# 320 rows of an output projection moved to five DMA engines

## The chip, the cores and the metric

The kernel runs on one core of a Trainium2 chip. The metric is the device time of one execution in microseconds (us), lower being better. "Span" is the time from the first to the last instruction in a profile or an execution; it leaves out about 2 us of the device time.

## The reference

A decode step: one token, 32 heads, a window of 4096 cached keys and values per head, and an output projection `wo`. A small gated branch (about 3.3 MB of weights) multiplies the result.

```python
W = min(4096, max(256, Sk // 4))
k = k_cache[:, :, Sk - W:, :]            # 32 heads x 4096 x 128, bf16
v = v_cache[:, :, Sk - W:, :]
scores = jnp.einsum("bhqd,bhkd->bhqk", q, k) * (Dh ** -0.5)
p = _softmax(scores, axis=-1)
o = jnp.einsum("bhqk,bhkd->bhqd", p, v)
s = o.transpose(0, 2, 1, 3).reshape(B, Sq, Hq * Dh) @ wo     # wo: 4096 x 512
return x + s * g
```

K and V are 1 MB (1024 KB) a head each, `wo` is 4: 68 such units, or 71 of the 79 million bytes that the kernel reads.

## The kernel before

All big loads go through one queue in program order. K head `i`, V head `i - 4` and now and then a block of `wo` follow one another. Each K or V tile is 128 partitions of 8 KB.

```python
def load(dst, src):
    return tc.keep_in_program_order(nc.sync.dma_start(out=dst, in_=src))
...
blocks = [(0, 8), (8, 8), (16, 8), (24, 4), (28, 4)]
...
def load_wo(i):
    h0, n = blocks[i]
    ...
    if i < last_block:                      # row p*n + t on partition p: one long packet a partition
        load(t[:], rows.rearrange("(p t) n -> p t n", p=P))
    else:                                   # head h, row p: 1 KB packets
        rows = rows.rearrange("(h p) n -> p h n", p=P)
        load(t[:, 0:n - 1, :], rows[:, 0:n - 1, :])
        load(t[:, n - 1, :], rows[:, n - 1, :])
...
for i in range(H + LAG):
    if i < H:
        k_head(i, load_kv(k_pool, A_k_cache, i))
    if i == LAG:                            # the small branch's weights are freed here,
        wts_guard.__exit__(None, None, None)
        v_pool = ctx.enter_context(tc.tile_pool(name="v", bufs=V_BUFS))   # V tiles lie behind what was allocated so far
    if i >= LAG:
        h = i - LAG
        v = load_kv(v_pool, A_v_cache, h)
        if h + 1 in (b[0] for b in blocks):
            load_wo(block_of[h])            # the block of heads 24-27 is issued at h = 27, behind the last K head
        if h == H - 1:
            load_wo(last_block)
        v_head(h, v)
```

For the long packets (8 KB for eight heads, 4 KB for four) a block's outputs have to be repacked (three DVE steps, one small matmul) before they meet `wo`. The tables for that are small constant tiles, one set for eight heads and one for four (`make_masks(8)`, `make_masks(4)`). In SBUF, where the loads put the tiles, the constants, the pool of K tiles, some small work pools and the pool of V tiles lie one behind the other: a later section turns on that.

## Time and profile before

| | before |
|---|---|
| median of 6 runs | 198.74 us (198.45 to 198.95) |
| span of the profiled run | 196.8 us |
| bytes read | 78.84 MB |
| DMA rate from 100 to 120 us | 423 GB/s |

The prediction below shows the lines that say that DMA sets the time. One more view is needed to follow what happened, the timeline of the tensor engine from the last K head on (columns: start, us, instruction, out<-in, count, and in brackets the idle time before and what ended it):

```profile
177.13 3.60 PE L271 MATMUL pt<-ident_bf,kv 128*128 128x128 bf16 x32 [1.49 <-DMA kv<-in_A_k_cache_dram]
...
184.07 0.27 PE L300 MATMUL den_ps<-pT,ones_bf 128*128 128x128 bf16 x1 [1.62 <-ACT pT L294]
184.72 0.17 PE L335 MATMUL ox_ps<-spread,to 128*128 128x16 bf16 x1 [0.38 <-DVE den L302]
...
185.90 1.01 PE L364 MATMUL oT<-pT,kv 128*128 128x1 bf16 x32
187.16 0.99 PE L364 MATMUL oT<-pT,kv 128*128 128x1 bf16 x32 [0.25 <-DVE o L367]
189.47 1.01 PE L364 MATMUL oT<-pT,kv 128*128 128x1 bf16 x32 [1.31 <-DMA kv<-in_A_v_cache_dram]
```

The last K head lands at 177.1. Transposes, scores and softmax take 6.9 us from there to the softmax denominators. Then the repacking (`ox_ps`) and V heads 28 and 29 run at PE's own pace, and heads 30 and 31 wait for their data. So two chains run to the end: **the DMA chain**, whose last V head lands at 191.89, and **the PE chain**, which starts at the last K head. Before the change the second has waits of 1.31 and 1.45 us in it. Without them head 31, at 1.25 us from head to head, would start at about 189.65 in place of 191.93 (an estimate): the PE chain can come some 2.3 us later before it ends the kernel.

The trace's own list of the chain that ended last, in order of time (start, us, what), agrees: it goes back through the last V head's transfer.

```profile
172.23 19.66 DMA kv<-in_A_v_cache_dram
191.89 0.05 issue
191.93 1.01 PE oT L364 x32
192.94 0.61 PE y_ps L135 x16
```

### The profile page before, as it was taken

The page shows a single profiled execution, that of the slowest core. Times are in us where ns is not written, and L with a number is a line of the kernel's source. Part 1 is how long each engine was busy: PE and PEld are TensorE (multiplying, and loading weights), DVE is VectorE, ACT ScalarE, POOL GpSimd, SP SyncE. Part 2 cuts the span into 40 slices and gives each one's busy share as a digit, 9 for nine tenths or more (in the row PEclk, how much of TensorE's full clock was granted, in tenths as well). Part 3 has the DMA queues.
Part 4 walks back from the last instruction along what each step waited for, and adds up shares of the span by engine and source line. Part 5 has one row for each costly group of instructions (what it writes and reads, how often), then busy time and mean ns, then how long its engine had stood idle before and what let it go on. Part 6 is the DMA issues. An engine that isn't in the chain of part 4 may idle for free.

```text
span 196.8 us, 5237 instructions
## 1 busy us (share of the span) xinstructions
PE 119.4 (61%) x2399; PEld 108.4 (55%) x2399; DVE 126.9 (64%) x140; ACT 69.3 (35%) x82; POOL 4.9 (3%) x17
## 2 busy tenths in 40 slices
PE   0315896851969474684829293756665654929443
PEld 0314745841969473583829292656565653929332
DVE  1225049998959993959387937959198929594301
ACT  2000329742565243070707070242525250707000
POOL 1011000000000000000000000000000000000000
PEclk9999999695585555576766667555555585575555
DMA  6999899999999999999999999999999999999960
GB/s 185 383 485 446 355 416 421 426 426 421 426 421 423 421 421 425 423 425 420 426 421 428 421 425 416 425 420 426 423 428 423 425 418 425 421 426 422 426 268 10
DMA packets 11349, 79.17 MB, mean 402 GB/s; under 512 B 1376, under 2 KB 1984, under 8 KB 2368
## 3 DMA queue, kind: packets, MB, share of 16 engines
q1 hardware_dynamic: 11176, 78.85, 96.3%
q8 instruction: 18, 0.29, 0.6%
q10 hardware_dynamic: 152, 0.00, 0.0%
q14 instruction: 3, 0.02, 0.0%
HBM read 78.84 MB, written 0.00 MB: 401 GB/s over the span
## 4 chain that ended last, share of the span: by engine, by line
DMA 71%; DVE 12%; issue 6%; PE 6%; ACT 2%; POOL 1%; SPq 0%; POOLq 0%
DMA kv<-in_A_v_cache_dram 40%; DMA kv<-in_A_k_cache_dram 30%; DVE sS L265 7%; DVE prod L262 3%; ACT kt L272 1%; PE a_ps L202 1%; PE qT_ps L221 1%; PE oT L364 1%; PE qb_ps L230 1%; PE h_ps L135 1%; PE y_ps L135 0%; PE ln_ps L140 0%; PE ln_ps L152 0%; ACT q_bc L232 0%; POOL ln_rstd_x L158 0%
## 5 line engine op out<-in xcount | busy, mean ns | idle before, releaser
L272 ACT COPY kt<-pt 128x1024 bf16<-128x1024 bf16 x64 | 60.2, 1025 | 73.0 <-PE pt L271 73.0
L265 DVE TENSOR_REDUCE sS<-prod 128x32 f32<-128x4096 bf16 x16 | 70.7, 4419 | 0.5
L271 PE MATMUL pt<-ident_bf,kv 128*128 128x128 bf16 x512 | 53.8, 298 | 18.2 <-DMA kv<-in_A_k_cache_dram 17.7
L271 PEld LDWEIGHTS <-kv 128*128 128x128 bf16 x512 | 49.8, 140 | 19.7 <-DMA kv<-in_A_k_cache_dram 18.7
L364 PEld LDWEIGHTS <-kv 128*128 128x128 bf16 x1024 | 30.0, 102 | 30.5 <-DMA kv<-in_A_v_cache_dram 22.8
L262 DVE TENSOR_TENSOR prod<-kv,q_bc 128x4096 bf16<-128x4096 bf16 x16 | 36.5, 2283 | 11.0 <-DMA kv<-in_A_k_cache_dram 8.8
L364 PE MATMUL oT<-pT,kv 128*128 128x1 bf16 x1024 | 32.6, 165 | 17.6 <-DMA kv<-in_A_v_cache_dram 17.3
L243 PE MATMUL sT<-qT_bf,kt 128*128 128x1 bf16 x512 | 20.4, 166 | 2.6 <-ACT kt L272 2.3
L243 PEld LDWEIGHTS <-kt 128*128 128x128 bf16 x512 | 18.3, 103 | 3.4 <-ACT kt L272 3.2
L300 PE MATMUL den_ps<-pT,ones_bf 128*128 128x128 bf16 x8 | 2.0, 253 | 16.9 <-ACT pT L294 16.9
L371 DVE TENSOR_TENSOR o<-oT,rden 128x4 bf16<-128x4 f32 x7 | 1.1, 162 | 17.3 <-PE oT L364 17.3
L294 ACT ACTIVATE pT<-e 128x128 bf16<-128x128 f32 x8 | 2.5, 309 | 16.5 <-DVE e L290 16.5
L140 PEld LDWEIGHTS ln_ps<-x_f,ones_f 128*128 128x128 f32 x4 | 1.0, 312 | 11.3 <-DVE x_f L182 6.4
L287 POOL PARTITION_ALL_REDUCE mb<-m x8 | 3.0, 373 | 162.5 <-DVE m L285 162.5
L205 ACT ACTIVATE a_bf<-a_ps 128x10 bf16<-128x10 f32 x1 | 0.2, 180 | 17.4 <-PE a_ps L202 17.4
L302 DVE TENSOR_REDUCE den<-den_ps 128x4 f32<-128x128 f32 x8 | 2.3, 292 | 5.5 <-PE den_ps L300 5.5
L135 PEld LDWEIGHTS <-ox 128*1 128x1 bf16 x112 | 2.5, 113 | 5.3 <-DVE ox L341 5.3
L367 DVE TENSOR_TENSOR o<-oT,rden 128x1 bf16<-128x1 f32 x4 | 0.6, 161 | 7.2 <-PE oT L364 7.2
L230 PE MATMUL qb_ps<-wq_sb,xn_rep 128*128 128x512 bf16 x16 | 5.2, 497 | 0.0
L135 PE MATMUL y_ps<-wo,ox 128*1 128x128 bf16 x112 | 3.7, 306 | 2.3 <-DVE ox L341 2.3
L140 PE MATMUL ln_ps<-x_f,ones_f 128*128 128x4 f32 x4 | 1.2, 365 | 5.9 <-DVE x_f L163 4.9
L290 DVE TENSOR_TENSOR e<-sS,mb 128x64 f32<-128x64 f32 x8 | 1.8, 224 | 3.9 <-POOL mb L287 3.9
(79 smaller groups left out, 48.2 us busy)
## 6 DMA issues: line engine op xcount, KB each, us to landing
kv<-in_A_k_cache_dram SPq DMA_DIRECT2D x32, 1024.0 KB, 19.7
kv<-in_A_v_cache_dram SPq DMA_DIRECT2D x32, 1024.0 KB, 19.7
wq_sb<-in_A_wq_dram SPq DMA_DIRECT2D x1, 4096.0 KB, 19.2
wo<-in_A_wo_dram SPq DMA_DIRECT2D x3, 1024.0 KB, 20.4
w_sb<-in_B_w_dram SPq DMA_DIRECT2D x1, 1376.0 KB, 7.9
w_sb<-in_B_w_dram SPq DMA_DIRECT2D x1, 1024.0 KB, 10.2
w_sb<-in_B_w_dram SPq DMA_DIRECT2D x1, 512.0 KB, 3.7
wo<-in_A_wo_dram SPq DMA_DIRECT2D x1, 512.0 KB, 19.8
```

The costliest lines, as they stand in the source:

```text
L135: nc.tensor.matmul(ps[32 * j:32 * j + 1, :], lhsT=col, rhs=w[0:k, j * P:(j + 1) * P], start=False, stop=last, skip_group_check=True)
L140: nc.tensor.matmul(ps[:], lhsT=ones_f[:], rhs=src_f, start=True, stop=True)
L230: nc.tensor.matmul(qb_ps[:], lhsT=xn_rep[:, c, :], rhs=wq_h[:, c, 2 * i:2 * i + 8:2, :], start=(c == 0), stop=(c == KC - 1))
L243: nc.tensor.matmul(sT[:, hl // 2, c:c + 1], lhsT=kt[:, c, :], rhs=qT_bf[:, h:h + 1], start=True, stop=True)
L262: nc.vector.tensor_tensor(out=prod[:], in0=kn[:], in1=q_bc[:, h // 2:h // 2 + 1, :].to_broadcast([P, NC, Dh]), op=ALU.mult)
L265: nc.vector.tensor_reduce(out=s["sS"][:, hl // 2, :], in_=prod[:], axis=AX.X, op=ALU.add)
L271: nc.tensor.transpose(pt[:, i, :], kn[:, b * 8 + i, :], ident_bf[:])
L272: nc.scalar.copy(out=kt[:, b * 8:(b + 1) * 8, :], in_=pt[:])
L287: nc.gpsimd.partition_all_reduce(mb[:], m1[:], channels=P, reduce_op=ReduceOp.max)
L294: nc.scalar.activation(out=pT[:], in_=e[:], func=ACT.Exp, scale=scale)
L302: nc.vector.tensor_reduce(out=den[:], in_=den_ps[:], axis=AX.X, op=ALU.add)
L364: nc.tensor.matmul(oT[:, k:k + 1], lhsT=v[:, c, :], rhs=s["pT"][:, hl % 2, hl // 2, c:c + 1], start=(c == 0), stop=(c == NC - 1))
```

## The change

The engines finish unevenly, so some rows of `wo` are to be carried by the engines that finish early. 320 rows (40 partitions of 8 KB) come as two transfers that only five engines are to serve; the other 704 rows of the last eight heads come in 1 KB packets on all engines. All of the last eight heads' outputs lie in one tile.

```diff
+NE = 5
-    make_masks(4)
+    few = const.tile([P, 2, 32], BF16, name="few")
+    ... a 0/1 matrix that spreads ox to the 40 partitions
+    def load_few():
+        t = wo_blk[few_block]
+        for c in range(2):
+            r0 = 8 * few_block * P + c * FEW // 2
+            load(t[32 * c:32 * c + 4 * NE],
+                 A_wo[r0:r0 + FEW // 2, :].rearrange("(b a t) n -> a b (t n)", b=4, a=NE))
...
+        if i == few_block:
+            of_ps = ps_misc.tile([64, n], FP32, tag="misc", name="of_ps")
+            nc.tensor.matmul(of_ps[:], lhsT=few[:].rearrange("p a b -> p (a b)"), rhs=ox[:], start=True, stop=True)
+            ox = sm_pool.tile([64, n], BF16, tag="of", bufs=1, name="of")
+            nc.vector.tensor_copy(out=ox[:], in_=of_ps[:])
...
-        if h == h0:
-            o_blk[i] = sm_pool.tile([P, n], BF16, tag="o", name="o")
+        if h % 8 == 0:
+            o_blk[i] = sm_pool.tile([P, 8], BF16, tag="o", name="o")
...
-            if h + 1 in (b[0] for b in blocks):
-                load_wo(block_of[h])
+            if h in (7, 15, 23):
+                load_wo((h + 1) // 8 - 1)
+            if h == H - 3 * G:                 # h = 20
+                load_few()
+            if h == H - G - 1:                 # h = 27
+                load(wo_rows[r_part:, 0, :], A_wo[h_part * P + r_part:(h_part + 1) * P, :])
+                load_rows(h_part + 1, H - G - h_part - 1)
             if h == H - 1:
-                load_wo(last_block)
+                load_rows(H - G, G - 1)
+                load_rows(H - 1, 1)
```

Cut: the pool tiles `wo_few` and `wo_rows` with two memsets, and renamed helpers.

More of the change, by code (lines that the diff above doesn't have):

```diff
@@ L233 @@
     make_masks(8)
-    make_masks(4)
+    few = const.tile([P, 2, 32], BF16, name="few")
+    nc.vector.memset(few[:], 0.0)
+    for c in range(2):
+        nc.vector.tensor_copy(
+            out=few[:, c, 0:4 * NE].rearrange("p (a b) -> p a b", b=4),
+            in_=ident_bf[:, 4 * NE * c:4 * NE * (c + 1)].rearrange("p (b a) -> p a b", b=4))
     st = {}
@@ L305, in softmax_den, with wo_row, load_rows @@
         s["rden"] = rden
-    blocks = [(0, 8), (8, 8), (16, 8), (24, 4), (28, 4)]
-    last_block = len(blocks) - 1
-    block_of = {h: i for i, (h0, n) in enumerate(blocks) for h in range(h0, h0 + n)}
+    few_block = H // 8 - 1
+    FEW = 8 * 8 * NE
+    h_part, r_part = divmod(24 * P + FEW, P)
+    assert h_part + 1 < H - G and 0 < r_part < P and r_part % 32 == 0
     o_blk, wo_blk = {}, {}
     def load_wo(i):
-        h0, n = blocks[i]
-        rows = A_wo[h0 * P:(h0 + n) * P, :]
-        if n == 8:
-            t = k_pool.tile([P, n, D], BF16, tag="kv", name="wo_8")
-        else:
-            t = v_pool.tile([P, n, D], BF16, tag=f"wo{i}", bufs=1, name="wo_4")
-        wo_blk[i] = t
-        if i < last_block:
-            load(t[:], rows.rearrange("(p t) n -> p t n", p=P))
-        else:
-            rows = rows.rearrange("(h p) n -> p h n", p=P)
-            load(t[:, 0:n - 1, :], rows[:, 0:n - 1, :])
-            load(t[:, n - 1, :], rows[:, n - 1, :])
+        t = k_pool.tile([P, 8, D], BF16, tag="kv", name="wo_8")
+        wo_blk[i] = t
+        load(t[:], A_wo[8 * i * P:8 * (i + 1) * P, :].rearrange("(p t) n -> p t n", p=P))
+    def load_few():
+        t = wo_blk[few_block]
+        for c in range(2):
+            r0 = 8 * few_block * P + c * FEW // 2
+            load(t[32 * c:32 * c + 4 * NE],
+                 A_wo[r0:r0 + FEW // 2, :].rearrange("(b a t) n -> a b (t n)", b=4, a=NE))
+    def wo_row(h):
+        return wo_rows[:, h - h_part, :]
+    def load_rows(h, n):
+        load(wo_rows[:, h - h_part:h - h_part + n, :],
+             A_wo[h * P:(h + n) * P, :].rearrange("(h p) n -> p h n", p=P))
     def repack(i):
-        n = blocks[i][1]
+        n = 8
         to, mt, mh = masks[n]
@@ L342, in repack, with apply_wo, apply_rows @@
                                     op=ALU.add)
-        o_blk[i] = ox
-    def apply_wo(i, t):
-        rows_add(y_ps, o_blk[i][:, t:t + 1], wo_blk[i][:, t, :],
-                 i == last_block and t == blocks[i][1] - 1)
+        if i == few_block:
+            of_ps = ps_misc.tile([64, n], FP32, tag="misc", name="of_ps")
+            nc.tensor.matmul(of_ps[:], lhsT=few[:].rearrange("p a b -> p (a b)"), rhs=ox[:],
+                             start=True, stop=True)
+            ox = sm_pool.tile([64, n], BF16, tag="of", bufs=1, name="of")
+            nc.vector.tensor_copy(out=ox[:], in_=of_ps[:])
+        return ox
+    def apply_wo(i, ox):
+        for t in range(8):
+            rows_add(y_ps, ox[:, t:t + 1], wo_blk[i][:, t, :], False)
+    def apply_rows(h):
+        rows_add(y_ps, o_blk[few_block][:, h % 8:h % 8 + 1], wo_row(h), h == H - 1)
     later = []
@@ L353, in v_head @@
         s = st[g]
-        i = block_of[h]
-        h0, n = blocks[i]
+        i = h // 8
         if hl == 0:
@@ L358, in v_head @@
             s["oT"] = ps_o.tile([P, G], FP32, tag="oT", name="oT")
-        if h == h0:
-            o_blk[i] = sm_pool.tile([P, n], BF16, tag="o", name="o")
+        if h % 8 == 0:
+            o_blk[i] = sm_pool.tile([P, 8], BF16, tag="o", name="o")
+            if i == few_block:
+                nc.vector.memset(o_blk[i][:], 0.0)
         k = 2 * (hl % 2) + hl // 2
@@ L365, in v_head @@
                              start=(c == 0), stop=(c == NC - 1))
-        if i == last_block:
-            nc.vector.tensor_tensor(out=o[:, h - h0:h - h0 + 1], in0=oT[:, k:k + 1],
+        if h >= H - G:
+            nc.vector.tensor_tensor(out=o[:, h % 8:h % 8 + 1], in0=oT[:, k:k + 1],
                                     in1=s["rden"][:, k:k + 1], op=ALU.mult)
@@ L371, in v_head @@
             nc.vector.tensor_tensor(
-                out=o[:, h - h0 - 3:h - h0 + 1].rearrange("p (a b) -> p b a", b=2),
+                out=o[:, h % 8 - 3:h % 8 + 1].rearrange("p (a b) -> p b a", b=2),
                 in0=oT[:].rearrange("p (b a) -> p b a", b=2),
@@ L377, in v_head, with step @@
             f()
-        if h == h0 + n - 1 and i < last_block:
-            def step(i=i, n=n):
-                repack(i)
-                later.append(lambda: [apply_wo(i, t) for t in range(n)])
+        if h in (7, 15, 23, H - G - 1):
+            def step(i=i):
+                ox = repack(i)
+                later.append(lambda: apply_wo(i, ox))
+                if i == few_block:
+                    later.append(lambda: [apply_rows(h) for h in range(h_part, H - G)])
             later.append(step)
@@ L391 @@
             v_pool = ctx.enter_context(tc.tile_pool(name="v", bufs=V_BUFS))
+            wo_blk[few_block] = v_pool.tile([64, 8, D], BF16, tag="wo_few", bufs=1, name="wo_few")
+            nc.gpsimd.memset(wo_blk[few_block][:], 0.0)
+            wo_rows = v_pool.tile([P, H - h_part, D], BF16, tag="wo_rows", bufs=1, name="wo_rows")
+            nc.gpsimd.memset(wo_rows[0:r_part, 0, :], 0.0)
         if i >= LAG:
@@ L394 @@
             v = load_kv(v_pool, A_v_cache, h)
-            if h + 1 in (b[0] for b in blocks):
-                load_wo(block_of[h])
+            if h in (7, 15, 23):
[5 more added lines that the diff above has]
+                load_rows(h_part + 1, H - G - h_part - 1)
             if h == H - 1:
-                load_wo(last_block)
+                load_rows(H - G, G - 1)
+                load_rows(H - 1, 1)
             v_head(h, v)
-    for t in range(blocks[last_block][1]):
-        apply_wo(last_block, t)
+    for h in range(H - G, H):
+        apply_rows(h)
     y = small.tile([P, P], FP32, name="y")
```

## The prediction

> **What bounds the kernel now.** I read the page's summary first, then the chain of work that ended last, then the windows of the last 24 us, then the DMA queue's own waits.
>
> ```profile
> DMA  6999899999999999999999999999999999999960
> GB/s 185 383 485 446 355 416 421 426 426 421 426 421 423 421 421 425 423 425 420 426 421 428 421 425 416 425 420 426 423 428 423 425 418 425 421 426 422 426 268 10
> ...
> q1 hardware_dynamic: 11176, 78.85, 96.3%
> q8 instruction: 18, 0.29, 0.6%
> ```
>
> From the second slice to the last but two the sixteen DMA engines are busy 90% or more, at about 424 GB/s, while DVE, the busiest compute engine, has 64% of the span. The bytes set the time: 78.85 MB at 424 GB/s are 186 us of a 196.8 us span.
>
> ```profile
> DMA 71%; DVE 12%; issue 6%; PE 6%; ACT 2%; POOL 1%; SPq 0%; POOLq 0%
> ...
> SPq L74 <- DMA kv<-in_A_v_cache_dram: 59.4, 28, 3.3
> SPq L74 <- DMA kv<-in_A_k_cache_dram: 59.2, 28, 2.9
> ```
>
> The chain says the same, and the queue's waits say how: an issue waits for the transfer eight issues before it, so about eight are in flight (19.7 us from issue to landing, one 1 MB head every 2.45 us). DVE's 12% of the chain lies before 52 us, under a full DMA queue; shortening it would gain nothing.
>
> What is left to win is in the last slices, so I cut them into windows (columns: stretch; busy us and instructions of PE, weight loads, DVE, ACT, POOL; clock; DMA share; GB/s):
>
> ```profile
> 186.00:188.00 2.00, 1.75 (x64) 1.76 (x63) 0.16 (x1) 0.00 (x0) 0.00 (x0) 0.50 1.03 425
> 188.00:189.00 1.00, 0.16 (x6) 0.07 (x3) 0.16 (x1) 0.00 (x0) 0.00 (x0) 0.50 0.88 351
> 189.00:190.00 1.00, 0.53 (x20) 0.54 (x21) 0.00 (x0) 0.00 (x0) 0.00 (x0) 0.50 0.58 224
> 190.00:191.00 1.00, 0.48 (x19) 0.40 (x15) 0.16 (x1) 0.00 (x0) 0.00 (x0) 0.50 0.58 202
> 191.00:192.00 1.00, 0.07 (x2) 0.07 (x3) 0.00 (x0) 0.00 (x0) 0.00 (x0) 0.50 0.24 85
> 192.00:193.00 1.00, 1.00 (x40) 0.98 (x44) 0.02 (x1) 0.00 (x0) 0.00 (x0) 0.50 0.12 41
> ```
>
> The bandwidth does not stop, it runs out in steps: half of the engines are done by 190 us, and from 192 to 193 a share of 0.12, two engines of sixteen, is all that works. The end hangs on those two:
>
> ```profile
> 191.93 1.01 PE L364 MATMUL oT<-pT,kv 128*128 128x1 bf16 x32 [1.45 <-DMA kv<-in_A_v_cache_dram]
> ...
> 192.93 0.60 PE L135 MATMUL y_ps<-wo,o 128*1 128x128 bf16 x16
> ...
> 193.58 0.29 DVE L404 TENSOR_TENSOR y<-y_ps,g_row 128x128 f32<-128x128 f32 x1 [0.43 <-PE y_ps L135]
> ```
>
> The last V head lands at 191.89, its 32 matmuls take 1.0 us, and the last rows of wo land at 193.18 and are used at once.
>
> The trace's semaphore records show each engine's part of a landing. The last wo transfer came in at 188.50, 188.64, 188.84, 189.28, 189.33, 189.60, 190.18, 190.82 (eight early engines), 191.52 to 191.82 (six) and 193.15, 193.18 (two). Their mean is 190.6: with equal finishes the end would come 2.6 us sooner, and that is all there is to gain. Following the engines back from landing to landing, all keep one pace, but after nearly every 16 KB packet of the instruction queue one of them falls back by 1.5 to 1.6 us for good. These jumps repeat after eight fetches, so I read them as eight engines in turn: two fetches each, and a third for the two late ones (fetches at 178.3 and 189.1). The other eight carry none.
>
> [...] 16 increments per big transfer, four packets of 256 B for the four-row load of x. [...] 16,384 B packets, mostly some 256 PE instructions apart. [...]
>
> **The change, part by part.** Before, head 24-27's wo (512 KB, packets of 4 KB) lay over all 16 engines ahead of the last four V heads, and head 28-31's as 1 KB packets behind them. After, 320 rows come as two transfers of 20 partitions x 8 KB. [...] The other 704 rows are 1 KB packets on all engines, 44 each, of which 12 come before the last four V heads and 32 behind.
> Costs per engine, from the spacing of landings: 8 packets of 8 KB 2.45 us; the 4 KB block 1.23 us; 32 packets of 1 KB 1.34 us (188.50 less 187.16), so 0.042 us each.
> - Before, every engine: 1.23 + 1.34 = 2.57 us.
> - After, engines 5 to 15: 44 x 0.042 = 1.86 us, **0.71 us less**.
> - After, engines 0 to 4: 2.45 + 1.86 = 4.31 us, **1.74 us more**.
>
> Who are engines 0 to 4? [...] in the load of w3 just after, four engines land at 8.81 to 9.13 and the rest by 8.31. Followed on, these four end in the early half, at about 189.3, 189.6, 190.2 and 190.8 (where two tracks cross, identity is my choice). For engine 4 I choose the early half as well, since the change is written for five.
> So: engines 0-4 end by 190.8 + 1.74 = 192.55; the two late ones at 193.18 - 0.71 = 192.47. The last V head: late engines 191.89 - 0.71 = 191.18, the slowest of 0-4 at 189.47 + 1.74 = 191.21. Both conditions of the end move by **0.63 to 0.68 us**, and the two groups meet, so nothing more is won.
>
> Compute: the instruction order shows 50 more PE instructions. They are 24 more y matmuls and one spreading matmul, with their weight loads. They stand between V heads 28 and 29, with one more DVE copy. The repacking (DVE and PE steps of 0.2 us each, some 1.6 us) and 40 y matmuls (at 0.6 us per 16, 1.5 us) now start after head 28. That puts head 29 at about 188.7 and head 30 at 189.7, done by 190.7, ahead of 191.2: hidden, by half a us. At the start four mask operations go and three come, equal. The two memsets on POOL (4096 elements; an estimate from 0.20 us for 128 elements, 0.10 for one: 3.4 us) fall in its idle stretch from 18 to 43 us.
>
> **Rivals.**
> (a) Engine 4 is one of the fetching eight. Then it ends at 191.5 to 191.8 plus 1.74, about 193.4, and the time is 198.9 us. Against: the author's choice of five. For: the trace of before cannot name engine 4.
> (b) The repacking after head 28 becomes the end. If V heads 29 to 31 queue behind a late repacking, PE rather than DMA would end the kernel; 0.5 us of room, so at worst a few tenths, 198.4 us.
> (c) The gain is hidden anyway, by small transfers that use up the eight places in flight, so that fast engines run dry. Two places with few bytes leave six heads, 14.7 us of work, against a spread of 4.7 us: no. Time would be 198.7 us.
> (d) The 50 PE instructions bring a fetch forward or add one. The fetch at 189.1 comes some 1 us sooner on the same engine; the next, at 197.8, falls after the end. If one more fell before it, an engine loses 1.55 us, perhaps one with room.
>
> **Range and chances.** 198.67 less 0.65 is 198.0 us. The runs of before spread over 0.35 us; (a) takes it to 198.9, a better balance than I follow gives 197.6. Range 197.5 to 198.8. A gain of 2% would be 4 us, more than the 2.6 us that perfect balance offers; a loss of 4 us has no source. So 98% within 2%.
>
> **What would show it.** In the changed kernel the two few-row transfers post five increments' worth of landings each. The DMA share stays high to about 190 us and then drops faster, without the long tail of two engines. The last V head lands near 191.2, the last wo row near 192.5, and y follows 0.4 us later. Instruction packets still number 18. The prediction is wrong if an engine of 0 to 4 ends after 193, if the last V head waits for PE instead of PE for it, or if the 1 KB packets cost more than 0.042 us each.

"Engines 0 to 4" is the name for the five that carry the few rows. With the cut terms the sum came to a gain of 0.63 to 0.68 us, 198.67 less 0.65, or 198.0 us. Its figures in us are read from the trace of before, but two of its terms stand as assumptions: that the two few-row transfers give five engines 8 packets of 8 KB each (2.45 us), and that four of those five are the engines that landed late at 8.81 to 9.13 us. The kernel after shows five landings for each of the two, 1.25 us a transfer, but no names.

## The result, and the profile after

| | before | after |
|---|---|---|
| median of 6 runs | 198.74 us (198.45 to 198.95) | 202.33 us (201.78 to 202.51) |
| span of the profiled run | 196.8 us | 200.1 us |
| last K head lands (its transposes start) | 177.13 | 180.47 |
| last V head lands | 191.89 | 193.79 |
| last rows of `wo` land | 193.18 | 195.21 |
| final product `y` starts | 193.58 | 196.76 |

The ratio is 1.0175 (95% interval 1.0158 to 1.0192). Ratios here are the mean time of one kernel's fast runs over that of the other's of the same rounds, so not quite the ratio of the medians. The change costs 3.6 us: still within 2%, but outside the predicted range of 197.5 to 198.8 and in the other direction. `y` starts 3.18 us later in the profiles; the rest of the 3.6 us lies outside that and is not assigned.

The page of the kernel after (summary in 40 slices, queues, chain):

```profile
DMA  6999899999999999999999999999999999999950
GB/s 193 385 463 439 364 414 414 422 418 419 424 416 414 421 416 421 416 422 414 419 418 421 418 421 416 421 416 421 414 422 421 416 421 418 416 420 382 412 215 0
...
q1 hardware_dynamic: 11306, 78.85, 96.1%
q8 instruction: 18, 0.29, 0.6%
...
DMA 74%; PE 12%; issue 9%; DVE 2%; POOL 1%; SPq 0%; ACT 0%; POOLq 0%
```

Bytes, busy share and instruction packets are the same, and yet the rate lies lower all the way, long before any transfer that the change touches (the first of those is issued at about 127 us). In equal stretches (us; busy us and count of PE, weight loads, DVE, ACT, POOL; clock; DMA share; GB/s), before and then after:

```profile
100.00:120.00 20.00, 12.51 (x257) 12.11 (x255) 14.53 (x11) 7.83 (x9) 0.37 (x1) 0.66 1.01 423
140.00:160.00 20.00, 12.97 (x274) 12.32 (x272) 15.01 (x13) 8.02 (x10) 0.37 (x1) 0.55 1.01 423
```

```profile
100.00:120.00 20.00, 12.82 (x257) 12.21 (x257) 14.52 (x10) 7.69 (x9) 0.00 (x0) 0.66 1.01 418
140.00:160.00 20.00, 11.59 (x248) 10.99 (x246) 14.63 (x12) 6.52 (x8) 0.37 (x1) 0.59 1.01 419
```

The engines are equally busy (the share of 1.01 is full) and move 1.2% less. The spacing of landings says which transfers: from 30 to 120 us the median spacing was 2.483 us for K heads and 2.438 us for V heads before, and 2.492 and 2.490 us after. V heads lost 0.052 us each, though nothing in their load was edited. (The spacing is that of the mean of a transfer's sixteen landings from the one before.)

The tail of the tensor engine after, from the last K head on:

```profile
180.47 3.59 PE L280 MATMUL pt<-ident_bf,kv 128*128 128x128 bf16 x32 [1.48 <-DMA kv<-in_A_k_cache_dram]
```

```profile
187.37 0.27 PE L309 MATMUL den_ps<-pT,ones_bf 128*128 128x128 bf16 x1 [1.58 <-ACT pT L303]
187.43 1.04 PE L389 MATMUL oT<-pT,kv 128*128 128x1 bf16 x32
188.98 0.21 PE L350 MATMUL ox_ps<-spread,to 128*128 128x64 bf16 x1 [0.51 <-DVE spread L347]
189.80 0.17 PE L360 MATMUL of_ps<-ox,few 128*64 128x8 bf16 x1 [0.61 <-DVE ox L356]
190.22 1.02 PE L136 MATMUL y_ps<-wo_few,of 64*1 64x128 bf16 x32 [0.25 <-DVE of L363]
191.17 0.38 PE L136 MATMUL y_ps<-wo_rows,o 128*1 128x128 bf16 x8
191.48 1.01 PE L389 MATMUL oT<-pT,kv 128*128 128x1 bf16 x32
192.75 0.99 PE L389 MATMUL oT<-pT,kv 128*128 128x1 bf16 x32 [0.25 <-DVE o L392]
194.00 0.75 PE L389 MATMUL oT<-pT,kv 128*128 128x1 bf16 x23 [0.25 <-DVE o L392]
195.77 0.40 PE L389 MATMUL oT<-pT,kv 128*128 128x1 bf16 x9 [1.02 <-issue]
196.11 0.60 PE L136 MATMUL y_ps<-wo_rows,o 128*1 128x128 bf16 x16
...
196.76 0.29 DVE L441 TENSOR_TENSOR y<-y_ps,g_row 128x128 f32<-128x128 f32 x1 [0.38 <-PE y_ps L136]
```

The last three V heads (191.48, 192.75, 194.00) wait for no DMA any more: PE comes from one to the next at its own pace. The list of the chain that ended last starts, in this tail, with the last *K* head, then PE's work:

```profile
160.57 19.86 DMA kv<-in_A_k_cache_dram
180.43 0.05 issue
180.47 3.59 PE pt L280 x32
```

Three things stand in the tail. The last K head is 3.3 us late. The repacking (`ox_ps`, `of_ps`) now stands between V heads 28 and 29 and holds the start of head 29 4.05 us behind that of head 28, of which the head's own matmuls are 1.0. And within the last head's 32 matmuls PE halts 1.02 us for nothing that the profile shows ("issue"). The trace of the instruction queue shows a 16 KB packet that starts at 193.24 and takes 1.07 us, so I read the halt as PE waiting for its next instructions; in the kernel before the last such packet in the tail comes at 189.10, and no halt follows.

The windows answer those of before (same columns):

```profile
189.00:190.00 1.00, 0.35 (x2) 0.13 (x1) 0.49 (x2) 0.00 (x0) 0.00 (x0) 0.50 1.03 414
190.00:191.00 1.00, 0.78 (x32) 0.73 (x32) 0.16 (x1) 0.00 (x0) 0.00 (x0) 0.50 0.81 335
191.00:192.00 1.00, 1.00 (x39) 0.62 (x28) 0.00 (x0) 0.00 (x0) 0.00 (x0) 0.50 0.76 302
192.00:193.00 1.00, 0.75 (x29) 0.69 (x27) 0.16 (x1) 0.00 (x0) 0.00 (x0) 0.50 0.85 301
193.00:194.00 1.00, 0.75 (x29) 0.76 (x27) 0.16 (x1) 0.00 (x0) 0.00 (x0) 0.50 0.41 130
194.00:195.00 1.00, 0.75 (x23) 0.66 (x22) 0.00 (x0) 0.00 (x0) 0.00 (x0) 0.50 0.09 29
```

The fall is faster, as the prediction asked for, though the share is not full: 0.76 to 0.85 from 190 to 193. Besides a single increment at 128.16, soon after its issue, the semaphore of the first few-row transfer gets five. They match five landings of the transfer before it plus 1.25 us:

```
prior 1 MB transfer, 16 landings:  140.71 140.91 141.04 141.78 142.00 142.13 142.21 142.21 142.34 142.41 142.45 143.08 143.87 143.88 143.89 144.16
few-row transfer, 5 landings:      143.03 143.26 143.38 143.70 144.31
```

Subtracting 1.25 leaves 141.78, 142.0, 142.13, 142.45 and 143.06: five engines, none of them among the last four, and not the three earliest, which keep ending about 2.7 us ahead of the rest.

### The profile page after: what moved, and what is told of

It reads as the page before. It is cut to its first block, busy times and chain, and to the rows that moved or that the text cites. A ratio compares the mean times of both kernels' runs of the same rounds, so it can differ in the third digit from the quotient of the medians.

```text
span 200.1 us, 5299 instructions
## 1 busy us (share of the span) xinstructions
PE 121.6 (61%) x2424; PEld 110.2 (55%) x2424; DVE 126.9 (63%) x141; ACT 69.3 (35%) x82; POOL 8.9 (4%) x19
## 4 chain that ended last, share of the span: by engine, by line
DMA 74%; PE 12%; issue 9%; DVE 2%; POOL 1%; SPq 0%; ACT 0%; POOLq 0%
DMA kv<-in_A_v_cache_dram 44%; DMA kv<-in_A_k_cache_dram 30%; PE qb_ps L231 3%; PE oT L389 2%; PE pt L280 2%; PE a_ps L203 1%; PE y_ps L136 1%; PE qT_ps L222 1%; PE h_ps L136 1%; PE sT L252 0%; SPq L75 0%; POOL ln_rstd_x L159 0%; POOL ln_rstd_z L159 0%; DVE o L392 0%; POOLq L470 0%
## 5 line engine op out<-in xcount | busy, mean ns | idle before, releaser
L280 PE MATMUL pt<-ident_bf,kv 128*128 128x128 bf16 x512 | 54.6, 302 | 19.7 <-DMA kv<-in_A_k_cache_dram 19.4
L280 PEld LDWEIGHTS <-kv 128*128 128x128 bf16 x512 | 50.7, 143 | 21.1 <-DMA kv<-in_A_k_cache_dram 20.5
L389 PEld LDWEIGHTS <-kv 128*128 128x128 bf16 x1024 | 30.2, 102 | 30.6 <-DMA kv<-in_A_v_cache_dram 21.3
L231 PE MATMUL qb_ps<-wq_sb,xn_rep 128*128 128x512 bf16 x16 | 5.7, 531 | 0.0
L233 ACT CAST q_bc<-qb_ps 128x512 bf16<-128x512 f32 x4 | 2.3, 586 | 5.3 <-PE qb_ps L231 5.3
```

What stands on the lines that cost most here:

```text
L231: nc.tensor.matmul(qb_ps[:], lhsT=xn_rep[:, c, :], rhs=wq_h[:, c, 2 * i:2 * i + 8:2, :], start=(c == 0), stop=(c == KC - 1))
L233: nc.scalar.copy(out=q_bc[:, i:i + 4, :], in_=qb_ps[:])
L280: nc.tensor.transpose(pt[:, i, :], kn[:, b * 8 + i, :], ident_bf[:])
L389: nc.tensor.matmul(oT[:, k:k + 1], lhsT=v[:, c, :], rhs=s["pT"][:, hl % 2, hl // 2, c:c + 1], start=(c == 0), stop=(c == NC - 1))
```

## What was to be told apart

Four theories came out of this reading; the texts sometimes refer to them by number.

1. **Placement.** The change removes the four-head tables (384 B a partition) and adds `few` (128 B) and `of` (32 B). K's pool, behind the constants, moves down by 256 B and V's, behind both, by 224 B. In the compiled programs the V tiles start at multiples of 512 B before, and 32 B past a multiple of 256 after; the K tiles start 64 B past one in both. The theory, an assumption here that runs 1, 2 and 11 were to test: where a tile starts in SBUF sets how long its load takes, and every V head (0.052 us, above), and the rows of `wo` that lie in V's pool, are slower by a little. The rival: a lower rate from something else, say the few-row transfers themselves.
2. **PE's halt** in the last head is a wait for instructions, whose place depends on PE's instruction count. (Between the ends of two 16 KB packets the trace of before has 256 matmuls and weight loads and that of after 258; these are medians, and single ones go from 121 to 441.)
3. **The shared tile of `o`.** Heads 28 to 31 write into the tile that the repacking of heads 24 to 27 reads, so the order of instructions puts the repacking behind head 28, after the denominators rather than ahead of them.
4. **The early issue of the few rows.** They are issued at h = 20, ahead of the last seven K heads; before, that block came behind the last K head. Five engines bring each of these K heads 2.5 us later than they otherwise would (two transfers of 1.25 us, as above), and PE starts on a K head only when all engines have landed: the last one's sixteen landings go from 175.56 to 180.43 us in the kernel after and PE starts at 180.47 (before, 173.77 to 177.09 and 177.13). PE's chain starts with the last one.

## The experiments

Fifteen runs were made, all correct. Unused "pad" tiles of a few bytes set where K and V lie; they are written once by a memset.

**1. After, with K and V aligned as before.** 256 B in the constants, 480 B ahead of the V pool: K tiles start at the very bytes of before, V tiles again at multiples of 512 B.

```diff
+    pad_v = prod_pool.tile([P, 240], BF16, tag="pad_v", name="pad_v")
+    nc.vector.memset(pad_v[:], 0.0)
...
+    pad_k = const.tile([P, 128], BF16, name="pad_k")
+    nc.vector.memset(pad_k[:], 0.0)
```

> The changed kernel, with two unused pads so that the K tiles start at the same SBUF byte as in the kernel before (64 above a multiple of 256) and the V tiles at a multiple of 512, as before (in the changed kernel they start 32 above one of 256). Theory 1 (the 8 KB packets of V take longer because of where the V tiles start): spacing of V landings falls from 2.49 to 2.44 us as in the kernel before, 32 x 0.05 = 1.7 us back, about 200.5 us; the PE stall of 1.0 us in the last V head stays. Rival (the slower packets come from the few-row transfers, the POOL memsets or the HBM side): spacing and time unchanged, 202.3.

Measured: 199.89 us (199.12 to 200.81), ratio 1.0011 (0.9949 to 1.0073), the profiled span 197.3 against 200.1 of after. Spacing K 2.481, V 2.438 us: those of before. The last V head lands at 191.71. Nothing but unused bytes was added, so the slower pace is placement.

```profile
178.88 3.60 PE L284 MATMUL pt<-ident_bf,kv 128*128 128x128 bf16 x32 [1.46 <-DMA kv<-in_A_k_cache_dram]
```

```profile
192.40 0.99 PE L393 MATMUL oT<-pT,kv 128*128 128x1 bf16 x32 [0.25 <-DVE o L396]
```

But the gain that was predicted is not there either: the last K head is still 1.75 us later than before, and the last V head, landed at 191.71, is taken up at 192.40 only when PE gets to it. The halt is gone as well (the late packet of instructions came at 190.51, well ahead of the last head), although PE's program is the same: whether it falls on the path depends on timing too (see run 13).

**2. Before, with the V tiles 32 B off.** One pad of 32 B in the kernel before, nothing else.

```diff
+    pad_v = prod_pool.tile([P, 16], BF16, tag="pad_v", name="pad_v")
+    nc.vector.memset(pad_v[:], 0.0)
```

> The kernel before, with one 32-byte pad ahead of the V pool, nothing else: V tiles start 32 above a multiple of 512. Theory 1: V landings 2.49 us apart instead of 2.44, 32 x 0.05 = 1.7 us lost, about 200.4 us. Rival (placement does not matter): 198.7.

Measured: 201.31 us (201.03 to 202.07), ratio 1.0086 (1.0029 to 1.0143). The runs of before in this call were disturbed (median 199.94, the two quiet ones 198.65 and 198.72), so I trust spans more: 199.1 to 199.4 in all four executions, against 196.9 in the quiet ones of before. Spacing K 2.491, V 2.490. 32 unused bytes cost 2.4 us:

```profile
194.37 1.01 PE L366 MATMUL oT<-pT,kv 128*128 128x1 bf16 x32 [1.73 <-DMA kv<-in_A_v_cache_dram]
```

The last V head comes 2.4 us later than before's 191.93, and PE waits for it. From the spacings: V's 0.052 us and K's 0.008 are 0.030 on average, over about 64 MB of transfers from the first V head on 1.9 us. Of the other 0.5 us, 0.3 is there in this profile when the first K head has landed (mean landing 24.25 against 23.95), before any V tile is loaded, so it is no cost of placement; 0.2 stays open.

**3. Before, with K placed too.** K and V tiles at multiples of 512 B (192 B and 320 B of pad).

> The kernel before, with pads so that K and V tiles both start at multiples of 512 (K starts 64 above one of 256 in the kernel before, V is placed already). Theory 1: K landings fall from 2.48 to 2.44 us apart, 36 transfers (32 K, 3 wo and one more) x 0.045 = 1.6 us gained, about 197.1 us. Rival (K's 2.48 has another cause): 198.7.

Measured: 198.83 us (197.88 to 200.83), ratio 0.994 (0.9864 to 1.0016): unclear, with a disturbed profile. Spacing K 2.450, V 2.447. It was run again as number 8.

**4. After, with PE's program shifted.** 64 one-column matmuls with zero weights (128 more PE instructions with their weight loads), spread over V heads 4 to 19.

```diff
+        if 4 <= h < 20:
+            for _ in range(4):
+                nc.tensor.matmul(y_ps[:, 0:1], lhsT=zero_bf[:], rhs=ident_bf[:, 0:1], start=False,
+                                 stop=False, skip_group_check=True)
```

> The changed kernel with 64 one-column matmuls of zero weights spread over V heads 4 to 19, where PE has room: 128 more PE instructions[...]. Theory 2 (in the changed kernel PE runs out of instructions inside the last V head, at 194.75 us, and waits 1.0 us for a 16 KB block[...]): the stall goes, about 201.3 us. Rival (the 1.0 us of unexplained idle is the crowded order of the tail itself, or a wait that the profile hides): the stall stays at the same matmul, 202.3.

Measured: 200.72 us (200.70 to 200.94), spans 198.9 to 199.1. More work, and over 1 us faster than after:

```profile
193.96 0.99 PE L389 MATMUL oT<-pT,kv 128*128 128x1 bf16 x32 [0.25 <-DVE o L392]
194.93 0.62 PE L136 MATMUL y_ps<-wo_rows,o 128*1 128x128 bf16 x16
...
195.60 0.29 DVE L445 TENSOR_TENSOR y<-y_ps,g_row 128x128 f32<-128x128 f32 x1 [0.45 <-PE y_ps L136]
```

The last head runs unbroken and `y` starts 1.16 us sooner than after's 196.76, with the spacing still at 2.49. So theory 2 holds, and the halt is worth 1.0 to 1.2 us.

**5. After, placed, with a tile of `o` of their own for heads 28 to 31.**

```diff
+        if h == H - G:
+            o_blk["last"] = sm_pool.tile([P, 8], BF16, tag="o", name="o_last")
-        oT, o = s["oT"], o_blk[i]
+        oT, o = s["oT"], o_blk["last" if h >= H - G else i]
```

> The changed kernel with V tiles placed as in the kernel before (as in the first experiment) and, besides, an o tile of its own for heads 28 to 31. Theory 3: in the changed kernel these four heads share o's tile with heads 24 to 27, so the repacking reads a tile that head 28 writes and must wait for head 28; that chain (matmuls of head 28, repacking, few-row matmuls, then heads 29, 30, 31 one after another with 0.25 us between) ended the first experiment at 193.98 us though its last V head had landed at 191.71. With its own tile the repacking starts before head 28, the last head waits for DMA again and y starts 1.7 us after its landing: 0.4 to 0.6 us less than the first experiment, and what is left against the kernel before is the balance of the engines alone: 198.0 us on a chip where the kernel before takes 198.7 (ratio 0.9965). Rival (the few-row transfers delay K31 and with it the softmax of the last group, and this delay sets the end whatever the tile): no better than the first experiment, ratio 1.00.

Measured: 200.02 us (199.62 to 200.94), ratio 1.0041 (1.0002 to 1.008); spans 197.1 to 197.3 but for one.

```profile
185.70 0.21 PE L354 MATMUL ox_ps<-spread,to 128*128 128x64 bf16 x1 [0.38 <-DVE den L315]
...
187.25 1.01 PE L396 MATMUL oT<-pT,kv 128*128 128x1 bf16 x32
...
191.85 0.75 PE L396 MATMUL oT<-pT,kv 128*128 128x1 bf16 x23 [0.25 <-DVE o_last L399]
193.00 0.40 PE L396 MATMUL oT<-pT,kv 128*128 128x1 bf16 x9 [0.40 <-issue]
```

The repacking is now ahead of head 28, as wanted, and the time did not improve: the last V head has landed at 191.16, yet PE reaches it at 191.85. Its chain starts with the last K head at 178.18, 1.05 us later than before. My third theory did not carry: from the denominators to the last V head PE takes 6.61 us in run 1 (185.79 to 192.40) and 6.75 here (185.10 to 191.85), so the tile's order costs nothing. What is longer than before is the work itself: the kernel before would need 5.6 us at its own pace (184.07 to the 189.65 estimated above). The halt is here too, 0.40 us. The delay of the K heads remained.

**6. As 5, with K placed too** (448 B and 288 B of pad).

> The same with the K tiles placed at multiples of 512 as well. Placement of K: 36 x 0.035 = 1.2 us less than the run with V alone placed (0.8 us if the quiet runs of the third experiment, 197.9 and 198.05, are right), about 197.0 us, below the placed kernel before by 0.65 us. If the few-row transfers gain nothing once placed: 197.9, equal to the placed kernel before.

Measured: 198.77 us (198.31 to 199.64), ratio 0.9977 (0.9937 to 1.0016). The pace is 2.45 us for both, and PE's chain is still the end (last K head 178.57, last V head landed 191.56, taken up 192.37; the profiled execution, with a span of 197.3, is the longest of the six, the others have 196.5 to 196.8).

**7. As 6, with `NE = 8`** (512 rows on 64 partitions, no partial row). It was meant to put the rows on eight engines; the landings of these transfers were not counted in runs 7 and 12.

> The same with 512 rows of wo on 64 partitions[...], and no rows left for heads 24 to 27. In the changed kernel three engines that are neither among 0-4 nor behind finish 2.8 us before the rest; if engines 0 to 7 are the eight without instruction fetches, then the other eight lose 1.23 us of transfers instead of 0.7 and the end comes 0.5 us sooner than with five: about 196.5 us. If one of 5 to 7 is a fetching engine, it ends 1.2 us later and the time is 198 or more.

Measured: 198.78 us (197.21 to 198.92), ratio 0.9959 (0.9913 to 1.0004), in two groups of spans: 195.4 to 195.5 and 196.9 to 197.1. In the profile, one of the second group, the packet of instructions at 189.69 met the engine that was last anyway and pushed it from 190.69 to 192.22. Inconclusive on `NE`.

**8. Run 3 again.**

> The third experiment again (kernel before, K and V at multiples of 512), because its profiled run was disturbed from 12 to 36 us (all engines slower in wq and the first K heads) and its timed runs were 197.9, 198.05, 199.6: 0.8 to 1.2 us below the kernel before if K's placement counts, equal to it if not.

Measured: 198.03 us (197.84 to 199.57), ratio 0.9955 (0.9913 to 0.9998), spans 196.1 to 196.3 undisturbed. Placing K as well gains some 0.7 us. I had expected more: K gains 0.031 us a head but V loses 0.008, so the pair gains only 0.011 us a transfer.

**9. As 5, with the few rows issued behind the last K head.**

```diff
-            if h == H - 3 * G:
+            if h == H - G - 1:
                 load_few()
```

> As the fifth experiment (changed kernel, V tiles placed as before, own o tile), with the two few-row transfers issued seven heads later: behind K31 and V27 instead of behind V20. Theory 4: issued early, they push every later transfer on engines 0 to 4 back by 2.5 us, so K31, whose last part those engines carry, lands 1.05 us later (178.18 against 177.13 us), and from K31 a fixed chain (transposes, scores, softmax, then PE's tail) runs to the end and hides the balance won on the engines. Issued late, K31 lands at 177.1 as in the kernel before, the last V head waits for its DMA again (landing 191.2, y 1.7 us later at 192.9 instead of 193.6): span 196.2 against 196.9 us, ratio 0.9965, which is what the prediction had. Rival (the engines' balance gains nothing, whatever K31 does): span 196.9 to 197.3, as in the fifth experiment.

Measured: 199.05 us (198.09 to 199.78), ratio 0.9989 (0.9945 to 1.0034). The profiled span is 196.3:

```profile
177.03 3.59 PE L284 MATMUL pt<-ident_bf,kv 128*128 128x128 bf16 x32 [1.46 <-DMA kv<-in_A_k_cache_dram]
...
187.37 1.01 PE L396 MATMUL oT<-pT,kv 128*128 128x1 bf16 x32
...
191.30 1.09 PE L396 MATMUL oT<-pT,kv 128*128 128x1 bf16 x32 [0.43 <-DMA kv<-in_A_v_cache_dram]
...
192.97 0.29 DVE L448 TENSOR_TENSOR y<-y_ps,g_row 128x128 f32<-128x128 f32 x1 [0.39 <-PE y_ps L140]
```

The last K head is back at 177.03, PE waits for the last V head again, and `y` starts 0.61 us sooner than before. That is the gain that the prediction worked out, at last visible. But the other five executions had spans of 196.8 to 197.2, as before has, so in the median it is the same as before. Run 9 has both the late issue and the tile of its own; since the tile alone brought nothing in run 5, the gain is the late issue's, but no run has that with the shared tile.

**10. As 9, with K placed too**: the version that this leads to.

> The same with K placed at multiples of 512 as well. The placed kernel before has a span of 196.1 to 196.3 us when undisturbed; theory 4: 195.5; if K31 was not what hid the gain: 196.3 to 196.7, as in the sixth experiment.

Measured: **197.30 us** (197.18 to 197.99), ratio 0.9906 (0.9865 to 0.9947). Spans 195.4 to 195.5, one 196.2. It is ahead of both kernels, of the one before by some 0.9% (clear of the noise, within 2%), and of the placed before of run 8 by 0.7 us in spans (196.1 to 196.3 there): the rebalancing is worth 0.7 us once nothing hides it.

```profile
190.45 1.01 PE L396 MATMUL oT<-pT,kv 128*128 128x1 bf16 x32 [0.94 <-DMA kv<-in_A_v_cache_dram]
```

**11. Before, with K at a multiple of 256 and V 128 B past one.**

> The kernel before with K tiles 256 above a multiple of 512 and V tiles 128 above a multiple of 256, for the spacing of landings alone. If what counts is a multiple of 256 bytes: K landings 2.44 to 2.45 us apart, V landings 2.48 to 2.49. If multiples of 512 are needed: both 2.48 to 2.49. If 64 or 128 were enough (K of the kernel before, at 64 above 256, says no): V 2.44.

Measured, one look: 199.29 us. Spacing K 2.438, V 2.473: here a multiple of 256 B was enough (K), and 128 B past one was not (V): it cost 0.035 us a head against the 0.052 of 32 B. Here K is the faster of the two, where before it was V.

**12. As 10, with `NE = 8`.**

> The seventh experiment (eight engines, 512 rows, K and V placed, own o tile) with the few-row transfers issued behind K31. Its spans fell into two groups, 195.4 and 197.0 us; in its profile the last instruction fetch met the slowest of the engines. If K31's delay matters with eight engines too, both groups fall, to 195.0 and 196.5; if the fetch alone decides, the groups stay at 195.4 and 197.0.

Measured: five fast executions of 197.39 to 200.25 us (median 198.71), ratio 0.9971 (0.9909 to 1.0034), spans from 195.6 to 198.4; a sixth, 201.69 us, was slow. In the profile a packet of instructions again met the slowest engine (190.64 to 192.25). `NE = 8` is not shown to be better than 5.

**13. After, as it is.** Was the halt an accident of one profile?

> The changed kernel itself, once more. If the halt belongs to it: a gap of about 1.0 us within the last V head's 32 matmuls, y near 196.8, span 199.6 to 200.1 us. If the halt was an accident of one profile: no gap, y near 195.6, span near 198.9. Landings of V heads 2.49 us apart either way.

Measured: 201.53 us, span 199.6; all seven executions of after have spans of 199.6 to 200.1. The halt is there again, at the same instruction, after 23 of the 32 matmuls:

```profile
195.28 0.40 PE L389 MATMUL oT<-pT,kv 128*128 128x1 bf16 x9 [0.79 <-issue]
```

The packets of PE's instruction queue tell why it comes and goes. In runs whose PE program has the same matmuls (us; the 24th matmul is the last head's):

| run | last packet landed | 24th matmul starts | between | halt |
|---|---|---|---|---|
| after | 194.31 | 195.77 | 1.47 | 1.02 |
| 13 | 193.78 | 195.28 | 1.50 | 0.79 |
| 5 | 191.58 | 193.00 | 1.41 | 0.40 |
| 9 | 190.57 | 191.99 | 1.42 | 0.06 |
| 1 | 191.44 | 193.02 | 1.58 | none |
| 14 | 192.51 | 194.16 | 1.65 | none |

PE goes on 1.4 to 1.5 us after the packet has landed; where it reaches the 24th matmul later than that, as in run 1, nothing is seen. Run 9 stands at the edge. (Runs 6, 10 and 15, without a halt, have 2.26, 1.69 and 1.46.)

**14. After with both repairs of the tail (own `o`, few rows late), placement left as it is.** Do the causes add up?

> The changed kernel with its own tile of o for heads 28 to 31 and the few-row transfers issued with the last rows of wo; placement left as it is (V tiles 32 above a multiple of 256). If placement and tail add up: the span of run 9 (196.3 to 197.2 us) plus the 2.0 to 2.4 us that the placement costs, 198.5 to 199.5 us, ratio to the kernel before 1.008 to 1.013; landings of V heads 2.49 us apart. The rival, that the placement matters only together with the tail's order, would have it at 197.5 us or less.

Measured: 200.62 us (200.50 to 200.99), ratio 1.0074 (1.0015 to 1.0133), spans 198.6 to 199.1, spacing 2.491 for both.

```profile
193.53 1.01 PE L392 MATMUL oT<-pT,kv 128*128 128x1 bf16 x32 [0.86 <-DMA kv<-in_A_v_cache_dram]
...
195.28 0.29 DVE L444 TENSOR_TENSOR y<-y_ps,g_row 128x128 f32<-128x128 f32 x1 [0.55 <-PE y_ps L136]
```

With the tail repaired the kernel is bound by DMA again, and is 2.3 us slower than run 9 (`y` at 195.28 against 192.97), which differs by the pads alone. They add up.

**15. Run 9 again**, for its other state.

> The kernel of run 9 again, for a look at its other state. If the span is 196.8 to 197.2 us and the cause is which engine the last fetch of instructions meets: the fetch at about 190 lies on one of the engines that end last, the last V head lands 0.6 to 0.9 us later than the 191.25 of run 9, and the tensor engine waits for it. If the cause is the tensor engine's own chain: the last V head lands at 191.3 as in run 9 and its matmuls start only after 191.9, without waiting for DMA.

Measured: 198.06 us, span 196.3, the last V head taken up at 191.29: the same state as in the first profile. The state of 196.8 to 197.2 was not caught, and its cause stays open. A packet landing 0.5 to 0.9 us later would make it, by run 13's table, but no profile shows that.

## Why the prediction was wrong

The step that failed first is the cost per engine: it took the pace of the untouched transfers for given, and each V head took 0.052 us more. The step "hidden, by half a us" failed second: PE's chain starts with the last K head, which the few rows delayed, and then halts for instructions. The gain of about 0.65 us was right. On the start of `y` in the profiles this is, step by step from before over runs 9 and 14 to after: 193.58 before, **-0.61** for the rebalancing with its tail repaired (run 9: 192.97), **+2.31** for placement (run 14: 195.28), **+1.48** for what else the change does to the tail (after: 196.76). Of the last, 1.0 to 1.2 us is PE's halt (run 4). The parts overlap, since the end is the later of two chains: repairing the tail's order, apart from the halt, is worth 1.0 us when the data come early (run 1 to run 9: 193.98 to 192.97) and 0.3 us when they come late (run 4 to run 14: 195.60 to 195.28).

- **"What bounds the kernel now": right.** It is DMA-bound before. (By their landings six engines, not half, are done by 190, and eight by 190.8.)
- **"Costs per engine, from the spacing of landings": the step that failed.** The change moved the V tiles off a multiple of 256 B, and each V head cost 2.490 in place of 2.438 us. Run 2 shows this alone: with 32 unused bytes in the kernel before, the profile is 2.4 us longer, 0.3 of it from its start. The prediction counted instructions and bytes; it did not compare where the tiles lie, which the compiled program would have told without a chip.
- **Five engines, all of the early half: right,** though no trace can name them as engines 0 to 4. Five engines land each few-row transfer (143.03 to 144.31 and 144.28 to 145.57 in the kernel after); in run 9 they are, by their landings, the fourth to the eighth of sixteen, the places that the prediction chose. The last V head was predicted for 191.2 and the last row for 192.5; in run 9, with pace and tail repaired, they land at 191.25 and 192.54. "The two groups meet" came true as well: the last three landings, 192.34, 192.49 and 192.54, are, followed back, two engines that a packet of instructions set back and the slowest of the five. (44 x 0.042 is 1.85, not 1.86; nothing hangs on it.)
- **"Hidden, by half a us" and rival (b): the mechanism was named, the size was wrong.** The prediction let head 29 follow at 188.7; it began at 191.48. The 4.05 us from head 28 to head 29 was not the surprise. The start was: the denominators came at 187.37 in place of 184.07. I asked what the few rows do to the last V heads and to the last row, and not what they do to the last K head, which they now precede. With the pace of before, the last K head comes 1.75 us later in run 1 and 1.05 in run 5, and not later in run 9, where they are issued late. In the kernel after, the K head is 3.3 us late and PE's work behind it 1.05 us longer (187.37 to 194.00, against 5.6 us); with 2.3 us of room that is the 2.07 us by which the last V head starts later (194.00 against 191.93).
- **Rival (d): asked the wrong engine.** The count of 18 instruction packets was right, and I looked only at what one does to the DMA engine that carries it. In after it came so late that PE halted for 1.02 us (0.79 in the second profile). What a packet costs the data did show in two runs: where the engine that fell back, by 1.5 to 1.6 us, was the last one (the profiles of runs 7 and 12), the span was 1.6 and 1.4 us above the shortest of the same kernel (197.0 against 195.4 and 195.6, which were not profiled).
- **Rival (a), engine 4 ends late:** the last row of `wo` lands at 195.21, past the 193 set as a sign of error; but 2.4 us of that is pace (194.92 in run 14 against 192.54 in run 9), and in run 9 all five start from the early half. So (a) is not what happened. The other two signs came as well: the last V head waited for PE, and 32 packets of 1 KB took 1.44 us in place of 1.34 (1.30 in run 9; medians over the sixteen engines).
- **"A loss of 4 us has no source": wrong by method.** I had bounded the gain by what the profile shows and the loss by what I had thought of. 3.6 us came from things that the profile of before cannot show.

Open: why run 9 has a second state; 0.2 us of run 2; by what mechanism the place in SBUF counts (only its effect was measured); and what sets when a packet of instructions comes.

## What to carry to other kernels

In a kernel bound by DMA, look at where its large tiles start before and after any edit that adds or drops a constant, and try them at multiples of 256 B, with small tiles behind them or a pad. Here a V head landed every 2.438 us at a multiple of 512 B, every 2.473 at 128 B past a multiple of 256 and every 2.490 at 32 B past one: up to 2%; in the whole kernel it was 2.3 us of 199 between runs 9 and 14, and 2.4 in run 2, 0.3 of it from its start. With both K and V placed, both took 2.45. When a transfer moves, ask what it now precedes, not only what it now follows; here the last K head was the victim. A gain that does not show may be there: repair the waits one at a time until the predicted number appears, and only then judge the idea.
